# Retention layer followed by a multiplicative feed-forward: heads of a pair swapped in the second output bank from the third step on, a marker copy on VectorE, and a new order of loads and of the first four steps

## Chip, cores and metric

The kernel runs on one core of one Trainium2 chip. The time is device microseconds (us) of one execution. Every duration below is in us unless it is marked ns.

## What is computed

```python
gamma = 1.0 - 2.0 ** (-5.0 - np.arange(H))            # B, H, S, D = 4, 8, 768, 64
for t in range(S):
    state = gamma * state + einsum('bhd,bhe->bhde', k[:, :, t], v[:, :, t])
    y[:, :, t] = einsum('bhd,bhde->bhe', q[:, :, t], state) / sqrt(D)
x = y.transpose(0, 2, 1, 3).reshape(B * S, H * D)      # 3072 tokens x 512
out = ((x @ w1) * (x @ w2)) @ w3 @ w_out               # 512 -> 1024 -> 1024 -> 512
```

## The kernel before, in words

**Tiling.** The recurrence is worked in 12 steps `n` (three for each of four batches), each of 256 tokens. Steps 0 and 1 (`n < EO = 2`) divide the 256 tokens into two chunks `g`, the later ones into four chunks `(s, g)`. `w3 @ w_out` is multiplied out once, into eight tiles W3O, before the first output.

**One step.** `cast` and `cast_v` (L261, L273) turn the loaded fp32 tiles into fp16; q and k are then transposed, by TensorE in `turn`/`turned` (L299, L306) for steps 0 to 2 and by a DMA in `dma_turn` (L292, issue at L295) for the others. `scores` (L319) and `mask` (L342) make the part inside a chunk; `kv` (L357) makes k times v, which `state` (L384) adds up from chunk to chunk. `inter` (L410, matmul L425) multiplies q with the state, `av` (L440, matmul L450) adds the masked scores times v into the same PSUM banks X[n, 0] and X[n, 1], and `x_out` (L456, L467 from step 2 on) scales with a table (YS or YN) and writes the fp16 tile XT. Head pair `a` holds two heads `r`; `inter`, `av`, `kv` and `scores` use 64x64 matmuls. A 64x64 matmul takes its weights from one half of the partitions (the row half of the array) and writes one half of the PSUM partitions (the column half). In `inter` the row half is `r` and so is the column half; the bank is `g`. In `av` the row half is `g`, the column half `r`. Between the two stands `fence` (L432, copy L438): ScalarE reads a few columns of both banks, so that `av` starts only when all of `inter` has been written.

**Feed-forward.** `a_unit` and `b_unit` (L499, L502; matmul L484) multiply XT with W1 and W2 in units of 256 columns. `a_evac` (L490, copy at L59) puts the first on ScalarE; `b_evac` (L494, L62) multiplies it with the second on VectorE into HT. `o_unit` (L528, matmul L532) multiplies HT with W3O, and `o_copy` (L540, L546) scales and writes out.

**What sets the order.** The program is written out by hand (`manual_schedule`): each engine runs its instructions strictly in the order in which the calls stand, and waits where one is not ready. L572 to L838 is a list of calls for the start, steps 0 to 2 and the attention of steps 3 and 4. From L877 on a loop runs over steps 3 to 11. Its first pass (n = 3) only calls `catch_up` (L859) and the feed-forward of step 3. A pass n > 3 is `inter(n)`, `fence(n)`, `ahead(n+1)` (scores and kv of the next step), `av(n)`, `x_out`, `ahead_out` (states and masks of the next step), the transposes of n + 2, loads and casts of n + 3, two `o_unit` of n - 1, and four `a_unit`/`b_unit` pairs.

**Queues.** All transfers, transposing ones too, are issued by SyncE in the order of the calls, on one queue. Loads go into 15 staging buffers `st`, reused in turn. The casts of the loop (`casts`, L842) are on GpSimd ("g"); in the list each call names its engine ("v" VectorE, "s" ScalarE, "g" GpSimd). The eight PSUM banks have the names S0, S1, X0, X1, K, F0, F1, F2; a call that names a bank waits until its last reader is done. `warm` (L562) is a run of matmuls on zeros.

The end of the list, which the prediction uses most:

```python
    o_copy(2, 0)
    state(4, 3)
    scores(4, ("X0", "K"))
    x_out(3, 1)
    o_unit(2, 1, ("F2",))
    cast("q", 5, "s")
    x_out(3, 0)
    state(4, 4)
    mask(4, 1)
    state(4, 5)
    o_copy(2, 1)
    cast("k", 5, "v")
    mask(4, 0)
    cast_v(5, "v")
```

Of the kernel before, what the change touches and what calls it, by code (L numbers as in the profile page):

```python
# [20 lines left out]
def kernel(  # L21
# [86 lines left out]
    def fetch(names):  # L108
# [12 lines left out]
        "r4 wo0 r1 r2 wo1 r5 wo2 r3 r6 k0 r7 wo3 q0 v0 r0 q1 k1 v1 w11 w13 w10 w12 w22 w23 w21 w20 "  # L121
        "v2 v3 k2 q2 k3 v4 q4"
# [10 lines left out]
    LGP = const.tile([128, NP], FP, name="LGP")  # L133
    keep = const.tile([128, 2, 128], FP, name="keep")
# [4 lines left out]
    def numbers():  # L139

        nc.gpsimd.iota(key_i[:, :, :], pattern=[[1, 2], [0, H]], base=1 - 128, channel_multiplier=2)
        nc.gpsimd.iota(
            col_i[:, :, :].rearrange("p g (t j) -> p g t j", t=2), pattern=[[128, 2], [1, 2], [2, 64]],
            base=1 - 128, channel_multiplier=0,
        )
        for h in range(H):
            r = (h % 2) * 64
            nc.gpsimd.memset(LGH[:, h : h + 1], -math.log(gam[h]))
            nc.gpsimd.memset(LGP[r : r + 64, h // 2 : h // 2 + 1], math.log(gam[h]))

# [65 lines left out]
    def late_tables():  # L216
        nc.scalar.activation(VN[:, :, :], vn_x[:, :, :], AF.Exp)
        for p in range(NP):
            nc.scalar.activation(YN[:, :, p, :, :], pos_f[:, :, :, :], AF.Exp, scale=LGP[:, p : p + 1])

# [157 lines left out]


# [30 lines left out]
    def inter(n, tags):  # L410
# [4 lines left out]
        for a in range(NP):  # L415
            for c in cs:
                if (n, c) not in TS:
                    continue
                for r in range(2):
                    if n < EO:  # L420
                        g, o, rhs = c, X[n, c][half(r), a, :], qT[n][half(r), :, a, half(c)]
                    else:
                        s, g = c
                        o, rhs = X[n, g][half(r), a, s * 64 : (s + 1) * 64], qchunk(n, r, a, s, g)
# [7 lines left out]
    def fence(n):  # L432

        for g in range(2):
            if (g, 0) in X[n]:
                s0 = 0 if n < EO or (n, (0, g)) in TS else 1
                t = att.tile([128, NP, 2 - s0], FP, tag=f"fence{g}", name="fence")
                nc.scalar.copy(t[:, :, :], X[n, g][:, :, :].rearrange("p a (s i) -> p a s i", s=2)[:, :, s0:, 0])  # L438

    def av(n):  # L440
        begun = X.pop(n)
        for a in range(NP):
            for t in range(2):
                for g, r in QUARTERS:
# [3 lines left out]
                    else:  # L448
                        o, rhs = X[n, g][half(r), a, t * 64 : (t + 1) * 64], am[n, None, r][half(g), a, t, :]
# [6 lines left out]
    def x_out(n, g):  # L456
# [9 lines left out]
        else:  # L466
            nc.vector.tensor_tensor(  # L467
                XT[n][:, :, :].rearrange("p a (s x) -> p (a s) x", s=2)[:, :, g * 64 : (g + 1) * 64].rearrange(
                    "p k (i t) -> p k t i", t=2
                ),  # L470
                x[:, :, :].rearrange("p a (s t i) -> p (a s) t i", s=2, t=2),
                YN[:, g, :, :, :].rearrange("p a s (t i) -> p (a s) t i", t=2), MULT,
            )
# [99 lines left out]
    warm(8)  # L573
    identity()
    numbers()
    keeps()
    arguments()
    tables()
    cast_w3(4, "v")
    step_decays()  # L580
    turn_w3(4, "S0")
    warm(4)
    late_numbers()
    cast_wo(0, "v")
    turned_w3(4, "s")
    late_arguments()
    w3_mm(4, 0, "S0", first=True)
    warm(7)
    cast_w3(1, "v")
    late_tables()  # L590
    turn_w3(1, "S1")
    warm(3)
    cast_w3(2, "g")
    turned_w3(1, "v")
    turn_w3(2, "X0")
    cast_wo(1, "g")
    w3_mm(1, 0, "S1", first=True)
    turned_w3(2, "s")
    w3_mm(1, 1)
    cast_w3(5, "v")  # L600
    w3_mm(4, 1)
    w3_mm(2, 1, "X0", first=True)
    w3_mm(2, 0)
    cast_wo(2, "g")
    turn_w3(5, "X1")
    turned_w3(5, "s")
    w3_mm(4, 2)
    w3_mm(1, 2)
    cast_w3(3, "s")
    w3_mm(2, 2)  # L610
    w3_mm(5, 2, "X1", first=True)
    cast_w3(6, "v")
    w3_mm(5, 0)
    turn_w3(3, "K")
    turn_w3(6, "F0")
    turned_w3(3, "v")
    w3_mm(5, 1)
    turned_w3(6, "v")
    w3_mm(3, 2, "K", first=True)
    w3_mm(3, 1)  # L620
    cast("k", 0, "v")
    w3_mm(6, 0, "F0", first=True)
    cast_w3(7, "g")
    w3_mm(6, 2)
    turn("k", 0, "F1")
    turn_w3(7, "F2")
    cast_wo(3, "v")
    w3_mm(3, 0)
    turned_w3(7, "s")
    turned("k", 0, "v")  # L630
    w3_mm(5, 3, last=True)
    w3_mm(1, 3, last=True)
    w3_out(5, "s")
    w3_mm(2, 3, last=True)
    cast("q", 0, "v")
    w3_mm(7, 2, "F1", first=True)
    w3_out(1, "s")
    w3_out(2, "v")
    turn("q", 0, "X1")
    w3_mm(4, 3, last=True)  # L640
    turned("q", 0, "v")
    w3_mm(7, 0)
    cast_v(0, "g")
    w3_mm(7, 3)
    w3_out(4, "v")
    scores(0, ("S1", "X0"), 0)
    scores(0, ("S0", "X1"), 1)
    cast_w3(0, "v")
    w3_mm(3, 3, last=True)
    w3_mm(6, 1)  # L650
    mask(0, 0, 1)
    w3_out(3, "s")
    turn_w3(0, "F2")
    mask(0, 1, 1)
    kv(0, ("S0", "K"))
    cast("q", 1, "g")
    mask(0, 0, 0)
    w3_mm(7, 1, last=True)
    w3_mm(6, 3, last=True)
    state(0, 1)  # L660
    w3_out(7, "s")
    turn("q", 1, "S1")
    mask(0, 1, 0)
    w3_out(6, "s")
    inter(0, ("S0", "X1"))
    cast("k", 1, "g")
    state(0, 2)
    fence(0)
    turned_w3(0, "v")
    av(0)  # L670
    state(0, 3)
    turned("q", 1, "v")
    turn("k", 1, "X0")
    w3_mm(0, 2, "K", first=True)
    cast_v(1, "g")
    turned("k", 1, "s")
    x_out(0, 0)
    w3_mm(0, 0)
    w3_mm(0, 3)
    x_out(0, 1)  # L680
    cast_w(W1, "w1", 1, "s")
    scores(1, ("S0", "S1"), 1)
    scores(1, ("X0", "F0"), 0)
    mask(1, 1, 1)
    w3_mm(0, 1, last=True)
    rows(W1, 0, 0, 1, ("X1", "F1"), first=True)
    mask(1, 1, 0)
    w3_out(0, "s")
    cast_w(W1, "w1", 3, "g")
    kv(1, ("S1", "F2"))  # L690
    mask(1, 0, 0)
    rows(W1, 0, 1, 1, ("K", "F0"), first=True)
    state(1, 1)
    rows(W1, 0, 0, 3)
    cast_w(W1, "w1", 0, "g")
    mask(1, 0, 1)
    inter(1, ("S1", "X0"))
    state(1, 2)
    rows(W1, 0, 1, 3)
    fence(1)  # L700
    state(1, 3)
    cast_w(W1, "w1", 2, "s")
    av(1)
    rows(W1, 0, 0, 0)
    x_out(1, 0)
    rows(W1, 0, 1, 0)
    cast_w(W2, "w2", 2, "g")
    x_out(1, 1)
    rows(W1, 0, 0, 2, last=True)
    rows(W1, 0, 1, 2, last=True)  # L710
    rows_out("a", 0, 0, 1, "s")
    rows(W1, 1, 0, 1, ("S0", "S1"), first=True)
    rows_out("a", 0, 1, 1, "s")
    rows(W2, 0, 0, 2, ("X0", "F1"), first=True)
    rows(W1, 1, 0, 0)
    rows_out("a", 0, 1, 0, "s")
    rows(W1, 1, 1, 1, ("F0", "F2"), first=True)
    cast_w(W2, "w2", 1, "g")
    cast_w(W2, "w2", 3, "s")
    rows(W1, 1, 0, 2)  # L720
    rows(W1, 1, 1, 3)
    rows_out("a", 0, 0, 0, "s")
    rows(W2, 0, 0, 3)
    cast_w(W2, "w2", 0, "v")
    rows(W2, 0, 0, 1)
    rows(W2, 0, 1, 3, ("X1", "K"), first=True)
    rows(W2, 0, 1, 2)
    rows(W2, 0, 1, 1)
    rows(W2, 0, 0, 0, last=True)
    cast_v(2, "g")  # L730
    rows(W1, 1, 1, 2)
    rows_out("b", 0, 0, 0)
    rows(W1, 1, 1, 0, last=True)
    rows(W2, 0, 1, 0, last=True)
    rows_out("b", 0, 0, 1)
    rows_out("a", 1, 1, 0, "s")
    rows(W1, 1, 0, 3, last=True)
    rows_out("a", 1, 1, 1, "v")
    rows(W2, 1, 0, 0, ("X0", "F0"), first=True)
    rows_out("a", 1, 0, 0, "s")  # L740
    rows(W2, 1, 0, 2)
    rows_out("b", 0, 1, 0)
    rows(W2, 1, 1, 1, ("S0", "F1"), first=True)
    rows_out("b", 0, 1, 1)
    rows(W2, 1, 1, 2)
    rows(W2, 1, 1, 3)
    cast_v(3, "v")
    rows(W2, 1, 0, 3)
    rows(W2, 1, 0, 1, last=True)
    cast("k", 2, "g")  # L750
    o_unit(0, 0, ("X1",))
    rows_out("a", 1, 0, 1, "v")
    rows_out("b", 1, 0, 0)
    rows_out("b", 1, 0, 1)
    turn("k", 2, "S1")
    o_copy(0, 0)
    cast("q", 2, "v")
    kv(2, ("X0", "K"))
    turned("k", 2, "s")
    rows(W2, 1, 1, 0, last=True)  # L760
    state(2, 1)
    turn("q", 2, "X1")
    state(2, 2)
    o_unit(0, 1, ("F0",))
    rows_out("b", 1, 1, 1)
    turned("q", 2, "s")
    state(2, 3)
    cast("k", 3, "s")
    rows_out("b", 1, 1, 0)
    inter(2, ("S1", "X0"))  # L770
    o_copy(0, 1)
    dma_turn("k", 3)
    fetch("q3 k4")
    scores(2, ("S0", "X1"))
    o_unit(1, 0, ("K",))
    mask(2, 0)
    cast_v(4, "g")
    fence(2)
    mask(2, 1)
    av(2)  # L780
    cast("q", 4, "s")
    kv(3, ("S0", "X1"))
    x_out(2, 1)
    o_unit(1, 1, ("F0",))
    o_copy(1, 0)
    dma_turn("q", 4)
    x_out(2, 0)
    state(3, 1)
    state(3, 2)
    ab["a", 2, 0] = two_blocks(W1, 2, 0, "S1")  # L790
    o_copy(1, 1)
    state(3, 3)
    ab["a", 2, 1] = two_blocks(W1, 2, 1, "X0")
    state(3, 4)
    a_evac(2, 0, ab["a", 2, 0])
    cast("q", 3, "g")
    ab["a", 2, 2] = two_blocks(W1, 2, 2, "S0")
    a_evac(2, 1, ab["a", 2, 1])
    state(3, 5)
    dma_turn("q", 3)  # L800
    ab["a", 2, 3] = two_blocks(W1, 2, 3, "S1")
    a_evac(2, 2, ab["a", 2, 2])
    ab["b", 2, 0] = two_blocks(W2, 2, 0, "S0")
    cast("k", 4, "v")
# [148 lines left out]
```

## Time and profile before

| what | value |
|---|---|
| median of 3 runs | 188.38 us (186.6 to 189.68) |
| the profiled execution, its own time | 187.29 us |
| its span, first to last instruction | 185.6 us |
| granted TensorE clock | 1.000 |
| busy: TensorE, its weight loads, VectorE, ScalarE, GpSimd | 175.7, 125.6, 100.2, 65.7, 56.9 us |
| moved by DMA | 40.76 MB, mean 220 GB/s |

The 1.69 us between 187.29 and 185.6 lie before the first and behind the last instruction. PE is TensorE's matmuls, PEld its weight loads, DVE VectorE, ACT ScalarE, POOL GpSimd, SPq the queue of SyncE that issues the DMAs. In a timeline each line is: start, duration, engine, source line, operation, output and inputs, shapes, count; in brackets the idle time of that engine before it, and what ended the wait. The chain of waits lists the work that ended last, in order of time: start, duration, what. Matmuls are pipelined, so a matmul's duration is longer than the time from its start to the next one's; where the text counts TensorE's work it goes by starts.

### The profile page before, as it was taken

To read this page: it belongs to the slowest core of one execution; us is meant where nothing else is said; L and a number is where in the kernel's file an instruction comes from. 1 tells how busy PE (TensorE), PEld (TensorE's weight loads), DVE (VectorE), ACT (ScalarE), POOL (GpSimd) and SP (SyncE) were. 2 spreads that over 40 slices of the span, in tenths; PEclk is the share of its full clock that TensorE was granted. 3 is DMA by queue.
4 is the path that set the end of the run, shared out by engine and by line. 5 is a ranking of instruction groups with operands and counts; after the bars stand their busy time and mean duration, and the time that the engine had idled before them with its cause. 6 is when DMAs were issued, how large, how long until landed. Compare 5 with 4: busy or idle time off the path is not lost.

```text
span 185.6 us, 5990 instructions
## 1 busy us (share of the span) xinstructions
PE 175.7 (95%) x2606; PEld 125.6 (68%) x2606; DVE 100.2 (54%) x171; ACT 65.7 (35%) x125; POOL 56.9 (31%) x85
## 2 busy tenths in 40 slices
PE   7999989999999988789999999999999999999993
PEld 2555546588765864675886868858678587685872
DVE  2424679625967188548347465373564745634220
ACT  5634414472082604221423323333243241331322
POOL 7860258644204301003425353532614500000000
PEclk9999999999999999999999999999999999999999
DMA  6999999999999989669999899999999996110303
GB/s 215 349 421 359 324 302 325 413 335 193 233 215 196 185 157 257 112 146 255 150 267 178 209 195 216 282 182 245 235 192 289 137 407 260 69 48 2 117 0 113
DMA packets 83578, 40.76 MB, mean 220 GB/s; under 512 B 61408, under 2 KB 78048, under 8 KB 83552
## 3 DMA queue, kind: packets, MB, share of 16 engines
q1 hardware_dynamic: 83552, 40.38, 93.3%
q8 instruction: 20, 0.33, 0.8%
q14 instruction: 6, 0.05, 0.1%
HBM read 29.36 MB, written 6.29 MB: 192 GB/s over the span
## 4 chain that ended last, share of the span: by engine, by line
PE 72%; DMA 16%; SPq 6%; POOL 2%; issue 1%; DVE 1%; ACT 0%; DVEq 0%; POOLq 0%
PE psF L484 32%; PE psF L532 19%; DMA st<-in_v_dram 9%; DMA st<-in_moe_w_dram 7%; SPq L95 3%; PE psF L514 3%; PE psX L425 3%; PE psS L484 2%; PE psX L514 2%; SPq L87 2%; PE psS L514 1%; PE psX L450 1%; PE psS L335 1%; DVE ht L62 1%; POOL v L62 1%
## 5 line engine op out<-in xcount | busy, mean ns | idle before, releaser
L484 PEld LDWEIGHTS <-w 128*128 128x128 f16 x640 | 62.6, 98 | 13.2 <-issue 4.0
L484 PE MATMUL psF<-xt,w 128*128 128x256 f16 x576 | 64.5, 273 | 2.6 <-DVE ht L62 1.9
L62 DVE TENSOR_TENSOR ht<-pa,psF 128x512 f16<-128x512 f32 x39 | 26.7, 686 | 40.5 <-PE psF L484 40.5
L532 PE MATMUL psF<-w3o,ht 128*128 128x512 f16 (+2 forms) x176 | 38.3, 370 | 0.0
L59 ACT COPY pa<-psF 128x512 f32<-128x512 f32 x39 | 22.8, 586 | 41.3 <-PE psF L484 36.7
L532 PEld LDWEIGHTS <-ht 128*128 128x128 f16 x200 | 18.4, 98 | 19.3
L546 ACT ACTIVATE st<-psF 128x512 f32<-128x512 f32 (+2 forms) x19 | 10.9, 575 | 31.0 <-PE psF L532 31.0
L62 POOL TENSOR_TENSOR v<-st,VN 128x1024 f16<-128x1024 f32 x8 | 15.2, 1903 | 17.7 <-DMA st<-in_v_dram 17.7
L59 POOL CAST k<-st 128x1024 f16<-128x1024 f32 x8 | 8.3, 1038 | 33.7 <-DMA st<-in_k_dram 33.7
L467 DVE TENSOR_TENSOR xt<-psX,YN 128x512 f16<-128x512 f32 x18 | 12.2, 727 | 7.4 <-PE psX L450 7.4
L514 PEld LDWEIGHTS <-w 128*128 128x128 f16 x128 | 12.0, 98 | 2.6 <-ACT w L59 0.7
L59 POOL CAST q<-st 128x1024 f16<-128x1024 f32 x8 | 8.3, 1041 | 10.3 <-DMA st<-in_q_dram 9.5
L352 DVE TENSOR_TENSOR am<-psS,keep 128x512 f16<-128x512 f32 x15 | 9.6, 680 | 1.2 <-PE psX L335 1.2
L248 PEld LDWEIGHTS <-w3t 128*128 128x128 f16 x64 | 5.6, 97 | 6.8 <-issue 0.8
L62 POOL TENSOR_TENSOR t<-s,GS 128x256 f16<-128x256 f32 x8 | 5.8, 730 | 13.1 <-DVE s L62 13.1
L514 PE MATMUL psF<-xt,w 128*128 128x256 f16 x56 | 9.7, 273 | 0.0
L565 PE MATMUL psX<-zeros 128*128 128x512 f16 x22 | 7.4, 484 | 1.3 <-DVE zeros L128 1.3
L425 PEld LDWEIGHTS <-t 64*64 64x64 f16 x320 | 6.2, 109 | 2.6 <-issue 2.1
L59 DVE CAST w3h<-st 128x1024 f16<-128x1024 f32 x5 | 4.1, 822 | 6.3 <-DMA st<-in_moe_w_dram 6.3
L425 PE MATMUL psX<-qT,t 64*64 64x64 f16 (+1 forms) x288 | 7.4, 195 | 0.0
L236 PEld LDWEIGHTS <-w3h 128*128 128x128 f16 x64 | 4.2, 103 | 3.5 <-DVE w3h L59 2.4
L484 PE MATMUL psS<-xt,w 128*128 128x256 f16 x48 | 5.7, 272 | 0.8 <-DVE ht L62 0.8
(129 smaller groups left out, 202.9 us busy)
## 6 DMA issues: line engine op xcount, KB each, us to landing
st<-in_moe_w_dram SPq DMA_DIRECT2D x16, 512.0 KB, 8.9
st<-in_q_dram SPq DMA_DIRECT2D x12, 512.0 KB, 5.9
st<-in_v_dram SPq DMA_DIRECT2D x20, 256.0 KB, 5.8
st<-in_k_dram SPq DMA_DIRECT2D x20, 256.0 KB, 5.0
out_dram<-st SPq DMA_DIRECT2D x8, 512.0 KB, 5.5
st<-in_moe_w_out_dram SPq DMA_DIRECT2D x4, 512.0 KB, 7.8
out_dram<-osb SPq DMA_DIRECT2D x3, 512.0 KB, 6.2
st<-in_k_dram SPq DMA_DIRECT2D x2, 512.0 KB, 10.1
```

What stands on the lines that cost most here:

```text
L59: {"v": nc.vector.tensor_copy, "g": nc.gpsimd.tensor_copy, "s": nc.scalar.copy}[eng](dst, src)
L62: (nc.vector if eng == "v" else nc.gpsimd).tensor_tensor(dst, a, b, op)
L95: nc.sync.dma_start(t[:, :], src[i * 128 : (i + 1) * 128, :])
L248: nc.tensor.matmul(acc[f][:, :], lhsT=w3t[f][:, g * 128 : (g + 1) * 128], rhs=WO[i][:, r, :], start=(first and r == 0), stop=(last and r = ...
L352: nc.vector.tensor_tensor(t[:, :, :, :].rearrange("p a s i -> p (a s) i"), ps[:, :, :, :].rearrange("p a s i -> p (a s) i"), keep64[:, :]. ...
L425: nc.tensor.matmul(o, lhsT=TS[n, c][half(r), a, :], rhs=rhs, start=((g, r) not in begun), stop=False, skip_group_check=True,)
L467: nc.vector.tensor_tensor(XT[n][:, :, :].rearrange("p a (s x) -> p (a s) x", s=2)[:, :, g * 64 : (g + 1) * 64].rearrange("p k (i t) -> p k ...
L484: nc.tensor.matmul(ps[:, i, :], lhsT=W[d][:, f * 128 : (f + 1) * 128], rhs=XT[n][:, d, :], start=(i == 0 and d == 0), stop=(i == 1 and d = ...
L514: nc.tensor.matmul(rows_ps[w, n, uh][j // 2][:, j % 2, :], lhsT=W[d][:, f * 128 : (f + 1) * 128], rhs=XT[n][:, d, :], start=(first and j % ...
L532: nc.tensor.matmul(ps[:, :], lhsT=HT[n][:, f, tb * 128 : (tb + 1) * 128], rhs=W3O[f][:, c0:c1], start=(f == 0), stop=(f == 7),)
L546: nc.scalar.activation(o_sb[n][:, tb, c0:c1], o_ps.pop((n, tb, c0, c1))[:, :], AF.Copy, scale=final_scale)
L565: nc.tensor.matmul(ps[:, :], lhsT=zeros[:, 0:128], rhs=zeros[:, :], start=True, stop=True)
```

## The change

- `place` swaps the two heads of a pair in bank g = 1 from step 2 on: in `inter` and `av` the column half there is 1 - r. `inter` then goes through four different pairs of row half and column half, one after the other, instead of two; within a chunk pair the order is now (g, r) = (0, 0), (1, 1), (0, 1), (1, 0).
- `x_out` puts the heads back: for g = 1 it becomes two VectorE instructions on 64 partitions each, for which the table YN is built with swapped rows (LGX: eight more small GpSimd memsets; YN in eight ScalarE activations of half the size).
- In the loop the `fence` copy of bank 1 moves to VectorE, and the last `b_evac` of a step is put behind the next step's `fence` in VectorE's order (`b_last`).
- `catch_up` no longer transposes step 5: both `dma_turn("q", 5)` and `dma_turn("k", 5)` now stand in the list.
- The order of the loads and the list of calls are new from end to end. The calls are nearly the same; `warm` matmuls go from 22 to 25, and several casts change their engine.

```diff
     fetch(
-        "r4 wo0 r1 r2 wo1 r5 wo2 r3 r6 k0 r7 wo3 q0 v0 r0 q1 k1 v1 w11 w13 w10 w12 w22 w23 w21 w20 "
-        "v2 v3 k2 q2 k3 v4 q4"
+        "r3 r6 wo0 r5 q0 r4 wo2 k0 wo1 wo3 r2 v0 r1 r7 k1 q1 v1 w12 w11 r0 w10 w13 w23 w20 w21 w22 "
+        "v2 q2 k2 q5 k3 k4 q3 q4 v3"
     )
...
+    def place(n, g, r):
+        return half(r if n < EO or g == 0 else 1 - r)
...
         for a in range(NP):
-            for c in cs:
-                if (n, c) not in TS:
-                    continue
-                for r in range(2):
+            for c, r in [(c, r) for c in cs for r in range(2)] if n < EO else [
+                ((s, g), r) for s in range(2) for g, r in ((0, 0), (1, 1), (0, 1), (1, 0))
+            ]:
+                if (n, c) in TS:
...
-                        o, rhs = X[n, g][half(r), a, s * 64 : (s + 1) * 64], qchunk(n, r, a, s, g)
+                        o, rhs = X[n, g][place(n, g, r), a, s * 64 : (s + 1) * 64], qchunk(n, r, a, s, g)
...
-                nc.scalar.copy(t[:, :, :], X[n, g][:, :, :].rearrange("p a (s i) -> p a s i", s=2)[:, :, s0:, 0])
+                copy(
+                    "s" if g == 0 else eng, t[:, :, :],
+                    X[n, g][:, :, :].rearrange("p a (s i) -> p a s i", s=2)[:, :, s0:, 0],
+                )
...
-                for g, r in QUARTERS:
+                for g, r in QUARTERS if n < EO else ((0, 0), (1, 0), (0, 1), (1, 1)):
...
+            for to in (slice(0, 128),) if g == 0 else (half(0), half(1)):
+                at = to if g == 0 else slice(64 - to.start, 128 - to.start)
+                nc.vector.tensor_tensor(
+                    xt[to].rearrange("p k (i t) -> p k t i", t=2),
+                    x[at, :, :].rearrange("p a (s t i) -> p (a s) t i", s=2, t=2),
+                    YN[at, g, :, :, :].rearrange("p a s (t i) -> p (a s) t i", t=2), MULT,
+                )
...
     def catch_up():
-        turns(LAST + 2)
         loads(LAST + 3)
         casts(LAST + 3)
...
             inter(n, ("X0", "X1"))
-            fence(n)
+            fence(n, "v")
+            b_last()
...
-            b_unit(n, u, tags[(2 * u + 1) % 3])
+            ps = two_blocks(W2, n, u, tags[(2 * u + 1) % 3])
+            b_last = functools.partial(b_evac, n, u, ps)
+            if u < 3 or n == NS - 1:
+                b_last()
```

The new list begins and ends like this (the middle is left out):

```python
    warm(8, "F2")
    identity()
    step_decays()
    late_numbers()
    numbers()
    warm(3, "F2")
    cast_w3(3, "v")
    turn_w3(3, "S0")
    keeps()
    late_arguments()
    warm(9, "F2")
    arguments()
    late_tables()
    turned_w3(3, "v")
    cast_w3(6, "g")
    cast_wo(0, "v")
    tables()
    turn_w3(6, "S0")
    cast_w3(5, "g")
    w3_mm(3, 0, "S1", first=True)
...
    cast("q", 5, "g")
...
    cast("k", 3, "s")
    rows_out("b", 1, 1, 0)
    inter(2, ("S0", "S1"))
    cast("k", 4, "g")
    scores(2, ("X1", "K"))
    o_copy(0, 0)
    dma_turn("k", 3)
    o_unit(1, 0, ("X0",))
    mask(2, 0)
    fence(2)
    mask(2, 1)
    cast("q", 3, "g")
    av(2)
    o_copy(1, 0)
    o_unit(1, 1, ("X1",))
    x_out(2, 1)
    dma_turn("q", 3)
    fetch("v4")
    x_out(2, 0)
    cast("q", 4, "v")
    ab["b", 2, 3] = two_blocks(W2, 2, 3, "S0")
    o_copy(1, 1)
    dma_turn("q", 4)
    dma_turn("k", 4)
    dma_turn("q", 5)
    fetch("k5 v5")
    ab["a", 2, 2] = two_blocks(W1, 2, 2, "S1")
    cast_v(3, "v")
    ab["a", 2, 1] = two_blocks(W1, 2, 1, "X0")
    a_evac(2, 2, ab["a", 2, 2])
    ab["b", 2, 1] = two_blocks(W2, 2, 1, "S1")
    a_evac(2, 1, ab["a", 2, 1])
    ab["a", 2, 0] = two_blocks(W1, 2, 0, "X0")
    b_evac(2, 1, ab["b", 2, 1])
    ab["b", 2, 2] = two_blocks(W2, 2, 2, "X1")
    a_evac(2, 0, ab["a", 2, 0])
    kv(3, ("S1", "X0"))
    b_evac(2, 2, ab["b", 2, 2])
    ab["a", 2, 3] = two_blocks(W1, 2, 3, "K")
    state(3, 1)
    cast_v(4, "g")
    ab["b", 2, 0] = two_blocks(W2, 2, 0, "X1")
    state(3, 2)
    a_evac(2, 3, ab["a", 2, 3])
    state(3, 3)
    b_evac(2, 3, ab["b", 2, 3])
    scores(3, ("K", "F0"))
    inter(3, ("S1", "F1"))
    mask(3, 0)
    o_unit(0, 1, ("F2",))
    fence(3)
    b_evac(2, 0, ab["b", 2, 0])
    mask(3, 1)
    o_unit(2, 0, ("S0",))
    state(3, 4)
    o_copy(0, 1)
    state(3, 5)
    kv(4, ("X0", "X1"))
    o_copy(2, 0)
    av(3)
    state(4, 1)
    scores(4, ("K", "F0"))
    cast("k", 5, "g")
    x_out(3, 1)
    o_unit(2, 1, ("S0",))
    x_out(3, 0)
    dma_turn("k", 5)
    mask(4, 1)
    cast_v(5, "g")
    o_copy(2, 1)
    mask(4, 0)
    state(4, 2)
    state(4, 3)
    state(4, 4)
    state(4, 5)
```

## Prediction

> **What bounds the kernel now.** I read the page first, then the timeline where TensorE is not full, then one pass of the loop, then the loads.
>
> The page's slices (40 of 4.64 us, busy tenths of TensorE and of the DMA engines):
>
> ```profile
> PE   7999989999999988789999999999999999999993
> ...
> DMA  6999999999999989669999899999999996110303
> ```
>
> TensorE is full except near the start and around slices 14 to 16; the DMA engines are full until about 74 us and after 83. From 84 to 182 the loop is bound by TensorE; up to 84, TensorE and the loads both bind.
>
> The timeline from 60 to 80 us, VectorE, ScalarE and TensorE:
>
> ```profile
> 65.43 0.69 DVE L59 CAST k<-st 128x1024 f16<-128x1024 f32 x1 [4.41 <-DMA st<-in_k_dram]
> ...
> 66.77 1.03 PE L484 MATMUL psS<-xt,w 128*128 128x256 f16 x8 [0.76 <-DVE ht L62]
> ...
> 72.06 1.05 ACT L59 CAST q<-st 128x1024 f16<-128x1024 f32 x1 [0.72 <-DMA st<-in_q_dram]
> ...
> 73.86 3.65 PE L484 MATMUL psF<-xt,w 128*128 128x256 f16 x32 [0.69 <-ACT osb L546]
> ...
> 75.69 0.69 DVE L59 CAST k<-st 128x1024 f16<-128x1024 f32 x1 [2.23 <-DMA st<-in_k_dram]
> ...
> 77.57 1.22 DVE L62 TENSOR_TENSOR v<-st,VN 128x1024 f16<-128x1024 f32 x1 [0.58 <-DMA st<-in_v_dram]
> ...
> 79.44 3.65 PE L484 MATMUL psF<-xt,w 128*128 128x256 f16 x32 [1.92 <-DVE ht L62]
> ```
>
> All three TensorE waits have one form: a cast of a late load (k4, q5, k5 and v5) stands in the strict order of VectorE or ScalarE, a PSUM reader stands behind it, and TensorE waits for the bank. From the first unit of step 2 (59.74) to inter(4) (83.03) are 23.3 us. By the distance of starts the work in it is 16 units of 0.874 (14.0), two o_unit of 1.74 (3.5) and 1.6 of attention: 19.1. So 4.2 us are waits.
>
> One loop pass, step 5, where inter, scores, kv and av follow each other:
>
> ```profile
> 95.00 0.63 PE L425 MATMUL psX<-qT,t 64*64 64x64 f16 x28
> 95.44 0.22 PE L335 MATMUL psS<-qT,kT 64*64 64x64 f16 x2
> ...
> 95.52 0.42 PE L335 MATMUL psS<-qT,kT 64*64 64x64 f16 x28
> 95.75 0.25 ACT L438 COPY fence<-psX 128x8 f32<-128x8 f32 x2 [0.94 <-PE psX L425]
> ...
> 95.78 0.20 PE L374 MATMUL psK<-v,k 64*64 64x64 f16 x1
> ...
> 101.94 0.69 DVE L62 TENSOR_TENSOR ht<-pa,psF 128x512 f16<-128x512 f32 x1 [1.04 <-PE psF L484]
> ```
>
> Inter takes 0.44 for 28 starts (16 ns each), the 28 scores from 95.52 to 95.78 take 9.3 ns each. VectorE has 1.04 us to spare before its first ht.
>
> The loads' landings, by the casts that waited for them:
>
> ```profile
> 49.13 1.04 POOL L59 CAST k<-st 128x1024 f16<-128x1024 f32 x1 [3.04 <-DMA st<-in_k_dram]
> ...
> 50.99 0.69 DVE L59 CAST q<-st 128x1024 f16<-128x1024 f32 x1 [0.39 <-DMA st<-in_q_dram]
> ...
> 56.14 1.90 POOL L62 TENSOR_TENSOR v<-st,VN 128x1024 f16<-128x1024 f32 x1 [5.97 <-DMA st<-in_v_dram]
> 58.98 1.05 ACT L59 CAST q<-st 128x1024 f16<-128x1024 f32 x1 [3.38 <-DMA st<-in_q_dram]
> ```
>
> They land one after another: a q costs 50.99 - 49.13 = 1.86; k3 and v4 cost 56.14 - 50.99 = 5.15, 2.58 each; q4 came 2.84 behind v4, 1.0 late, with k3's transpose issued at 55.00.
>
> **The change, part by part.** *The start.* GpSimd has more ahead of its first cast: from the identity's end (1.37) GS 1.94, late numbers 1.61, iotas 0.45, 24 small memsets (16 took 1.50, so 2.25), keep 1.98, so it casts r6 at 9.6 and r5 at 10.7 (1.04 each). VectorE's argument tables wait for LGH until 7.7, then it turns out r3. TensorE's 20 warm-ups end at about 8.3 and it has nothing until r6 is cast (10.7). Before, three W3 tiles were turned by 10.9; now two by 11.3. I then walked the new list with the rows' durations (VectorE 0.61 to 0.69 per cast, ScalarE 1.01, turn 0.44, w3_mm 0.44, landings by position in the queue, 1.25 to 1.3 per weight block as between 10.55 and 13.11). The chain cast, turn, turned out, product has no slack up to r7, and the first W1 row group starts at 34.4. Set against before at 35.25, where its own last wait in this part ends, it lacks W3 tile 0 (turn 0.44, eight products of 0.218) and two row groups (0.87) and is ahead by inter(1) (0.35): 2.7 of work, so it is 34.4 + 2.7 - 35.25 = 1.85 late.
>
> *34.4 to the first unit of step 2.* Before needed 24.49 from 35.25 to 59.74. The new list adds those 2.7 and puts off o_unit(0, 1) and kv(3) (1.74 + 0.30); inter(2) saves 0.13; the third x_out part makes XT come 0.3 behind o_unit(1, 1). 34.4 + 24.49 + 2.7 - 2.04 - 0.13 + 0.3 = 59.7.
>
> *59.7 to inter(4).* The work is 19.1 + 2.04 - 0.1 = 21.0: inter(4) at 80.7 if nothing waits. What can wait now: k4, q5, k5 and v5 are cast on GpSimd, with no PSUM reader behind them, so the three old waits go. But cast q4 and v3 are on VectorE ahead of four b_evac. v3 is ninth instead of second: v2 q2 k2 q5 k3 k4 q3 is 4 x 2.58 + 3 x 1.86 = 15.9 against 14.76 for the six up to v4 at 56.14, so 57.3; q4 59.1, v3 61.7, and 1.0 later if k3's transpose runs among them as before: 62.7. Its cast ends at 63.9, b_evac(2, 1) at 64.5, just when kv(3) wants bank S1 (64.6). No cost, no slack. Next late are the transposes on SyncE's queue, k3 q3 (v4) q4 k4 q5. Scores(4) needs k4's. Before they started without waiting at 70.91, behind the same transfers but without q5's load (1.86): 72.8 at most. From there 0.3 + o_unit(2, 1) 1.74 + eight units 6.99 gives inter(4) at 81.8. Ends 80.7 and 81.8; I take 81.5, nearer to the loads, which fill their engines. Gain 83.03 - 81.5 = 1.5. K5's transpose no longer stands with q5's behind v5: scores(5) wants it at about 82. A transpose costs 1.46 of the queue (v7 waited for at 100.53, k8 at 106.03, two transposes and a k between: (5.50 - 2.58) / 2); 72.8 + 1.46 (q5) + 2 x 2.58 (k5, v5) = 79.4 for v5, whose GpSimd cast (1.9) ends at 81.3, and 80.9 for k5's transpose: cover of 0.7 us, less if the loads slip.
>
> *The loop, steps 4 to 11.* Inter and scores together take 0.78 (95.00 to 95.78); 64 starts at 9.3 ns are 0.60. Bounds: 0 (the old rate) and 0.18, 0.13 in steps 6 and 9, which have 24 matmuls: at most 1.3. The new order visits all four quadrants like scores, so I take 1.0 in all. The fence needs inter's last start + 0.19 + 0.06 + 0.17 = 0.42, less than scores and kv behind it (0.6): no wait, and its move to VectorE gains nothing but in step 11. VectorE pays 0.62 (third x_out part; back-to-back distance) of its 1.04: 0.4 left. b_last starts about 0.6 later and ends near 96.4; o_unit reads its two rows of HT with the seventh matmul, 6 x 0.218 after 95.95: hidden. If that cover goes, a late ht holds a bank that is wanted 1.75 later: still nothing. Warm-ups, fence and ACT's halved tables otherwise lie in waits.
>
> A rule that speaks against the loop's gain: by the Trainium skill, "TensorE: Matmul & The Clock Gate", Part 3, a weight load overlaps a running matmul only if its row group differs. The new order's row halves are 0, 1, 1, 0, the scores' 0, 1, 0, 1. By that rule the loop gains nothing and the sum ends 1.0 higher. No row here shows such an order.
>
> The same page (Part 1) throttles TensorE after an idle window of about 3.4 us; the idle after the warm-ups is 2.4, below it. In this trace the first eight warm matmuls took 3.60, the last seven 1.67. If the gate closed, an estimate from the page would be some 1.7 more in the start.
>
> **Sum.** 187.29 (the profiled execution, 1.69 of it outside the span) - 1.5 - 1.0 = 184.8. That execution was 1.1 quicker than the median, 188.38, from which it would be 185.9. I say 185.3.
>
> **Rivals.**
> *More gain*: the loads keep ahead and the quadrants reach the scores' rate: (83.03 - 80.7) + 1.3 = 3.6, 184.2 by the same middle, less if the start is quicker than walked. For it: DMA is only at 6 tenths in slices 16 and 17. Against: full before.
> *Heads swapped, no faster*: the 16 ns stay; only the 1.5 is left: 186.3. For it: neighbours share a row or column half, as never before.
> *The start is not made up*: another 1.5 lost in the walk's chain before 34.4, inter(4) at 83: 186.8. For it: chain without slack.
> *Slower*: v3's cast holds VectorE. It stands ahead of b_evac(2, 1), which frees S1 for kv(3); each us that v3 lands after 62.8 is one on the path. From 65.3 on the whole gain of 2.5 is gone. If transposes get in front of the last two loads at their dearest (4.8 from issue to landing, the median), v3 lands at 67.5 and the time is 190. Against: it was issued ahead of them.
>
> **How the numbers follow.** Chances: forecast 0.45 (own range 184.2 to 186.4), more gain 0.22, no faster 0.12, start 0.11, slower 0.10. A measurement tells about 2% from no change: 3.8 us, so faster is below 184.6. That takes most of the second case and a quarter of the first: 0.32. Slower by 2% (192.2) needs the last case and a bad start: 0.08. Range: down past 184.2 by 1.4 (the start's uncertainty), up to where half of the last case is in: 182.8 to 188.8.
>
> **What would show it.** Right: first W1 row group near 34.4; no idle over 0.3 on TensorE from there to 58; no PE wait for ht behind a cast between 59 and 80; scores(4) near 72.5 waiting for kT; inter(4) near 81.5; inter's starts 10 to 13 ns apart; loop passes of 11.85 instead of 12.0. Wrong: v3's cast after 64, VectorE's spare time before the first ht at zero, a fence that TensorE waits for, or a loop pass no shorter.

## The result, and the profile after

The kernel with the change takes 186.13 us (median of 20 runs, 184.52 to 187.09), the kernel before 188.33 (20 runs beside them, 186.43 to 190.65). Five of the runs of before are in a slower state that none of after's shows; the ratio leaves them out and is 0.9905, 95% interval 0.9876 to 0.9935. So the change gains about 1.8 us or 1%: clear of zero, and inside the 2% that was called no change. The profiled execution took 186.98 (span 185.2). Against the profiled one of before, 187.29, that is only 0.3, because after's lies 0.85 above its median and before's 1.0 below. So the two traces show where time is won and lost, and the runs the size of the gain; what spreads the runs of before over 4 us was not looked for.

The slices of after's page (4.63 us each):

```profile
PE   7769999999999899999999999989999999999993
...
PEclk9969999999999999999999999999999999999999
DMA  5999999999989999699899899999999990110203
```

Two things are new. The dip of TensorE around slices 14 to 16 has gone, and in the third slice the granted clock is at 6 tenths, where before had full speed throughout. The mean over the execution is 0.990. That is the usual case: 15 of after's 20 runs have a mean clock of 0.988 to 0.991, five of 0.999 to 1.000.

The start on TensorE, from after's timeline:

```profile
11.03 1.04 PE L241 MATMUL psS<-ident,w3h 128*128 128x128 f16 x8 [2.85 <-POOL w3h L60]
```

The granted clock us by us, from after's windows (start and end, length, then busy us of TensorE, its weight loads, VectorE, ScalarE and GpSimd, granted clock, DMA share, GB/s):

```profile
10.00:11.00 1.00, 0.00 (x0) 0.00 (x0) 0.00 (x0) 1.00 (x5) 1.00 (x2) 0.88 1.02 401
11.00:12.00 1.00, 0.97 (x9) 0.97 (x10) 0.00 (x0) 1.00 (x3) 0.96 (x1) 0.50 0.98 371
...
13.00:14.00 1.00, 1.00 (x6) 0.47 (x5) 0.99 (x2) 0.00 (x0) 0.00 (x0) 0.50 1.17 338
14.00:15.00 1.00, 1.00 (x13) 0.76 (x12) 0.00 (x0) 0.43 (x1) 0.00 (x0) 0.92 1.04 401
```

TensorE stands idle for 2.85 us until r6 is cast, and in this idle time the clock goes to half. From the 0.88 and the 0.92 the half clock lasts from 10.76 to 14.16, 3.4 us. The turn of r6 takes 1.04 for eight transposes, against 0.61 at full clock.

The part from 58 to 80 us (timeline):

```profile
58.81 2.21 DVE L482 TENSOR_TENSOR xt<-psS,YN 64x512 f16<-64x512 f32 x3 [0.99 <-PE psS L462]
...
60.91 0.68 DVE L60 CAST q<-st 128x1024 f16<-128x1024 f32 x1
...
61.07 1.92 PE L497 MATMUL psS<-xt,w 128*128 128x256 f16 x16 [0.59 <-DVE xt L482]
61.50 1.22 DVE L63 TENSOR_TENSOR v<-st,VN 128x1024 f16<-128x1024 f32 x1
```

VectorE's timeline at the end of that stretch:

```profile
73.40 0.42 DVE L63 TENSOR_TENSOR t<-psX,t 128x256 f16<-128x256 f32 x1 [2.04 <-PE psX L379]
73.86 1.47 DVE L482 TENSOR_TENSOR xt<-psF,YN 64x512 f16<-64x512 f32 x2
75.34 0.72 DVE L482 TENSOR_TENSOR xt<-psS,YN 128x512 f16<-128x512 f32 x1
```

And TensorE's first unit of step 3, behind them:

```profile
76.12 7.15 PE L497 MATMUL psF<-xt,w 128*128 128x256 f16 x64 [0.42 <-DVE xt L482]
```

The three old waits (0.76, 0.69, 1.92) are gone. In their place TensorE waits twice for `x_out`, 0.59 and 0.42: three VectorE instructions instead of two stand between `av` and the first unit of steps 2 and 3. The cast of the slower rival, v3's at 61.50, shows no wait for its load at all. And no load is what the end of this stretch waits for; k5's cast was waiting for TensorE:

```profile
73.30 1.04 POOL L60 CAST k<-st 128x1024 f16<-128x1024 f32 x1 [1.06 <-PE psX L379]
76.61 1.90 POOL L63 TENSOR_TENSOR v<-st,VN 128x1024 f16<-128x1024 f32 x1 [2.27 <-DMA st<-in_v_dram]
```

These two are on GpSimd, and nothing on the path stands behind them. inter(4) starts at 83.20, before at 83.03. The timeline of before:

```profile
83.03 0.63 PE L425 MATMUL psX<-qT,t 64*64 64x64 f16 x28
```

And of after:

```profile
83.20 0.45 PE L434 MATMUL psX<-qT,t 64*64 64x64 f16 x32
```

One pass of the loop, step 5 (timeline):

```profile
94.95 0.45 PE L434 MATMUL psX<-qT,t 64*64 64x64 f16 x32
...
95.23 0.55 PE L340 MATMUL psS<-qT,kT 64*64 64x64 f16 x32
...
95.57 0.17 DVE L60 COPY fence<-psX 128x8 f32<-128x8 f32 x1 [1.50 <-PE psX L434]
...
96.67 2.21 DVE L482 TENSOR_TENSOR xt<-psX,YN 128x512 f16<-128x512 f32 x3 [0.34 <-PE psX L462]
...
101.83 0.67 DVE L63 TENSOR_TENSOR ht<-pa,psF 128x512 f16<-128x512 f32 x1
```

The 32 starts of `inter` now take 95.23 - 94.95 = 0.28, 8.7 ns each, where 28 took 0.44. The fence makes nobody wait here. The first ht of the pass shows no wait any more: VectorE's spare 1.04 is used up.

The chain of waits for the pass of step 7 (start, duration, what):

```profile
118.80 0.38 PE psX L434 x32
119.17 0.29 PE psS L340 x30
...
120.00 1.19 PE psF L545 x5
121.19 0.82 issue
122.01 2.55 PE psF L545 x11
124.56 5.46 PE psF L497 x50
```

In the middle of an `o_unit` TensorE stands for 0.82 us without waiting for anything that the profile shows ("issue"). The passes last 11.89, 11.89, 12.75, 11.88, 11.75, 11.74 and 11.70 (first unit to first unit, from step 4 on); the 12.75 is this one. Before they took 12.01, 12.01, 11.98, 11.98, 11.94, 11.97 and 11.98.

The end of the loop is read from the last 24 output products, the x24 group at the end of the chain. Before:

```profile
178.93 3.49 PE psF L532 x24
```

After:

```profile
178.61 3.49 PE psF L545 x24
```

From inter(4) to this group it is 178.93 - 83.03 = 95.90 before and 178.61 - 83.20 = 95.41 after, or 94.59 without the 0.82. So the loop gains 1.31 and one stop takes 0.82 of it back.

### The profile page after: what moved, and what is told of

Same layout as the page of the kernel before. It is cut to its first block, busy times and chain, and to the rows that moved or that the text cites. A ratio compares the mean times of both kernels' runs of the same rounds, so it can differ in the third digit from the quotient of the medians.

```text
span 185.2 us, 5993 instructions
## 1 busy us (share of the span) xinstructions
PE 174.4 (94%) x2609; PEld 124.3 (67%) x2609; DVE 112.3 (61%) x191; ACT 67.0 (36%) x122; POOL 53.5 (29%) x90
## 4 chain that ended last, share of the span: by engine, by line
PE 85%; DVE 5%; POOL 5%; issue 2%; ACT 1%; DVEq 0%; POOLq 0%; ACTq 0%
PE psF L497 34%; PE psF L545 19%; PE psX L253 4%; PE psS L253 3%; PE psS L527 3%; PE psF L527 2%; DVE xt L482 2%; PE psX L497 2%; PE psX L434 2%; PE psX L462 2%; PE psS L497 2%; DVE am L351 1%; PE psS L340 1%; PE psX L527 1%; PE psX L545 1%
## 5 line engine op out<-in xcount | busy, mean ns | idle before, releaser
L497 PE MATMUL psF<-xt,w 128*128 128x256 f16 x576 | 64.3, 273 | 0.4 <-DVE xt L482 0.4
L545 PE MATMUL psF<-w3o,ht 128*128 128x512 f16 (+2 forms) x168 | 36.6, 369 | 0.8 <-issue 0.8
L60 ACT COPY pa<-psF 128x512 f32<-128x512 f32 x37 | 21.7, 586 | 34.6 <-PE psF L497 34.4
L482 DVE TENSOR_TENSOR xt<-psX,YN 64x512 f16<-64x512 f32 (+1 forms) x24 | 17.4, 727 | 1.7 <-PE psX L462 1.4
L60 POOL CAST q<-st 128x1024 f16<-128x1024 f32 x9 | 9.6, 1069 | 16.2 <-DMA st<-in_q_dram 14.7
L253 PE MATMUL psX<-wo,w3t 128*128 128x512 f16 x32 | 8.9, 380 | 0.4 <-ACT w3t L60 0.2
L578 PE MATMUL psF<-zeros 128*128 128x512 f16 x25 | 7.5, 442 | 1.3 <-DVE zeros L129 1.3
L527 PE MATMUL psS<-xt,w 128*128 128x256 f16 x48 | 8.2, 273 | 0.4 <-DVE w L60 0.4
L60 DVE COPY fence<-psX 128x8 f32<-128x8 f32 x8 | 1.3, 166 | 11.5 <-PE psX L434 11.5
L253 PE MATMUL psS<-wo,w3t 128*128 128x512 f16 x24 | 7.5, 421 | 0.0
L527 PE MATMUL psF<-xt,w 128*128 128x256 f16 x40 | 6.5, 273 | 0.0
```

Source lines behind the costliest of these rows:

```text
L60: {"v": nc.vector.tensor_copy, "g": nc.gpsimd.tensor_copy, "s": nc.scalar.copy}[eng](dst, src)
L253: nc.tensor.matmul(acc[f][:, :], lhsT=w3t[f][:, g * 128 : (g + 1) * 128], rhs=WO[i][:, r, :], start=(first and r == 0), stop=(last and r = ...
L482: nc.vector.tensor_tensor(xt[to].rearrange("p k (i t) -> p k t i", t=2), x[at, :, :].rearrange("p a (s t i) -> p (a s) t i", s=2, t=2), YN ...
L497: nc.tensor.matmul(ps[:, i, :], lhsT=W[d][:, f * 128 : (f + 1) * 128], rhs=XT[n][:, d, :], start=(i == 0 and d == 0), stop=(i == 1 and d = ...
L527: nc.tensor.matmul(rows_ps[w, n, uh][j // 2][:, j % 2, :], lhsT=W[d][:, f * 128 : (f + 1) * 128], rhs=XT[n][:, d, :], start=(first and j % ...
L545: nc.tensor.matmul(ps[:, :], lhsT=HT[n][:, f, tb * 128 : (tb + 1) * 128], rhs=W3O[f][:, c0:c1], start=(f == 0), stop=(f == 7),)
```

## The experiments

The theory after this reading: the swap gains 1.3 in the loop, and its third `x_out` part costs 1.0 of that in steps 2 and 3, so what the whole change gains is the list. Rivals: the list's gain is lost in the start and the swap is what pays; the wait at 121.19 belongs to the swap; the fast `inter` comes from its order of row halves, not from the four quadrants. The runs stand in three groups, each on one chip: e1 to e4, e5 to e7, and e8 to e10, with medians of the kernel before of 188.34 (23 runs), 187.77 (11) and 188.72 (11). Between groups the ratios to before are compared.

**e1: the swap alone.** Before's loads, list of calls and `catch_up`; after's functions and loop.

> The list of calls and the loads of before, with the swap, the split x_out, the fence on VectorE and the late b_evac of the change. Theory (the swap gives about 1.2 us in the loop, the new list the rest): loop passes of 11.85 instead of 12.0 us, inter's 32 starts in 0.28 us, inter(4) within 0.4 us of 83.0, time 1.0 to 1.4 us below the kernel before. Rival (the new list alone brings the gain, the swap's longer VectorE work eats what inter saves): time within 0.3 us of before.

Measured: 187.3 (12 runs), ratio 0.9968 [0.9932, 1.0004]. The old waits are all there (waits, TensorE):

```profile
PE psF L497 <- DVE ht L63: 1.7, 1, 1.7
PE psF L497 <- ACT osb L559: 0.9, 1, 0.9
...
PE psS L497 <- DVE ht L63: 0.4, 1, 0.4
```

With them stands a wait of 0.3 for xt. Seven passes take 83.30 instead of 83.87, 0.57 less, with an "issue" wait of 0.23 among them. The swap by itself is at most a gain of 0.7%. By the ratio that is 0.6 us, between what the theory (1.0 to 1.4) and the rival (0.3) had asked for, so this run decides for neither.

**e2: the list alone.** After, with the swap taken out everywhere.

```diff
     def place(n, g, r):
-        return half(r if n < EO or g == 0 else 1 - r)
+        return half(r)
...
-            for c, r in [(c, r) for c in cs for r in range(2)] if n < EO else [
-                ((s, g), r) for s in range(2) for g, r in ((0, 0), (1, 1), (0, 1), (1, 0))
-            ]:
+            for c, r in [(c, r) for c in cs for r in range(2)]:
...
-            for to in (slice(0, 128),) if g == 0 else (half(0), half(1)):
+            for to in (slice(0, 128),):
```

> The changed kernel with only the swap undone: inter's old order and halves, x_out in two instructions, YN from LGP; the new list, the fence on VectorE and the late b_evac stay. Theory: loop passes back at 12.0 us, inter's 32 starts in 0.44 us, but XT of steps 2 and 3 some 0.6 us earlier each, so inter(4) near 82.4 instead of 83.3; time 0.5 to 1.0 us below the kernel before. Rival (the swap gives nothing): time equal to the changed kernel or below, 1.8 us or more under before.

Measured: 185.35 (6 runs), ratio 0.989 [0.9848, 0.9933]: the list alone gives what the whole change gives, as the rival had it. Its timeline of TensorE:

```profile
59.74 1.91 PE L495 MATMUL psS<-xt,w 128*128 128x256 f16 x16
...
81.39 0.63 PE L432 MATMUL psX<-qT,t 64*64 64x64 f16 x28
```

No wait for xt; inter(4) at 81.39, which is 1.64 before the kernel before and 1.81 before after. The passes are the old ones, about 12.0, so the swap does give something in the loop, which the rival had denied. The granted clock of the profiled execution is 1.000: the idle time behind the warm-ups was 2.22 here, because the warm-ups ended later.

**e3: the clock gate kept open.** `warm(9, "F2")` becomes `warm(21, "F2")` in after.

> The changed kernel with 21 instead of 9 warm-up matmuls ahead of the wait for r6, 2.6 us of work in an idle stretch. Theory (the idle from 8.2 to 11.0 closed TensorE's clock: granted 0.83 from 10 to 20 us, transposes of 0.13 us instead of 0.055): granted clock 1.00 from 10 to 20 us, first W1 row group near 34.4 instead of 35.25, time 0.3 to 0.9 us below the changed kernel. Rival (VectorE's masks and casts set when the row groups can go on): first row group earlier, but the third group of W1, after w10's cast, still at 38.5, time unchanged.

Measured: 185.67 (12 runs), ratio 0.9897 [0.9863, 0.993]. The clock from 10 to 20 us is 1.00. The first W1 row group comes at 34.92 instead of 35.25, the first unit of step 2 at 60.38 instead of 61.07: the closed gate cost 0.7 on that path. The third row group comes at 37.79, not at 38.5 as the rival had it. The time, 0.46 under after's, is not told apart from it, but after's own runs agree: the 15 with a clock of 0.988 to 0.991 have a median of 186.3, the five with 0.999 or more 185.5, and none of the 12 runs of e3 is below 0.999. An "issue" wait of 0.96 falls in the pass of step 7 here too.

**e4: the keep table later.** In after, GpSimd makes the mask table `keep` behind its first two casts.

```diff
-    keeps()
     late_arguments()
...
     cast_w3(5, "g")
+    keeps()
```

> The changed kernel with GpSimd's keep table (2.2 us) made behind its casts of r6 and r5 instead of ahead of them. Theory (GpSimd's first cast at 9.9 sets the whole start): r6 cast at 7.7, its turn at 8.8, clock 1.00 throughout, first W1 row group at 33 to 34, inter(4) 1.0 to 2.0 us earlier, time 0.8 to 1.8 us below the changed kernel. Rival (from there on the loads' landings set the pace): r5 and q0 follow no earlier, first row group not before 34.5, time within 0.4 us of the changed kernel.

Measured: 183.44 (6 runs), ratio 0.9788 [0.9747, 0.983]: 2.7 below after's median, 2.2 by the ratios, more than the theory's 0.8 to 1.8. Timeline of TensorE:

```profile
9.09 0.62 PE L241 MATMUL psS<-ident,w3h 128*128 128x128 f16 x8 [0.93 <-POOL w3h L60]
...
32.67 0.39 PE L527 MATMUL psS<-xt,w 128*128 128x256 f16 x2
```

The idle time is 0.93 instead of 2.85, the clock stays at 1.0, the first W1 row group comes at 32.67, 2.6 earlier, and inter(4) at 80.43, 2.8 earlier. What limited the start was GpSimd's queue ahead of its first cast, not the loads; some 0.7 of the gain is the clock that now stays open (e3). The waits for xt are unchanged (0.59 and 0.42), the "issue" wait is 0.09.

**e5: the swap only from step 4 on.** e4, with steps 2 and 3 unswapped; the loop's rows get a second table, YX, and steps 2 and 3 use YN in one `x_out` instruction per bank.

```diff
-        return half(r if n < EO or g == 0 else 1 - r)
+        return half(r if n < 4 or g == 0 else 1 - r)
...
-            for to in (slice(0, 128),) if g == 0 else (half(0), half(1)):
+            swap = g == 1 and n >= 4
+            for to in (half(0), half(1)) if swap else (slice(0, 128),):
```

> The kernel with the keep table behind the casts, and the swap from step 4 on only: steps 2 and 3 keep inter's old order and a single x_out instruction for bank 1 (a table YN unswapped for them, a second one, YX, for the others). Theory (the split x_out costs 1.0 to 1.3 us where TensorE waits for XT in the list, steps 2 and 3, and nothing in the loop): no TensorE wait for xt, step 3's first unit at 72.0 to 72.5 instead of 73.35, loop passes as short as with the swap everywhere (11.75 to 11.9), time 0.8 to 1.2 us below e4_keeps. Rival (those waits hide another, a load or a bank): step 3's first unit moves by less than 0.4 us.

Measured: 183.13 (6 runs), ratio 0.9761 [0.9715, 0.9808]. The waits for xt are gone, but the first unit of step 3 comes only 0.62 earlier than in e4 (72.73), not the 0.85 and more that was expected: the second table lengthens ScalarE's part of the start by 0.4 (its tables end at 10.7 instead of 10.3), and inter(2) starts at 53.34 instead of 52.94. From there to inter(4) it is 26.47 instead of 27.49, and that is the 1.02 of the two waits. An "issue" wait of 0.38 is in this run. By the ratios the time is 0.5 below e4, less than the 0.8 to 1.2 of the theory and not told apart from it. v3's cast now does wait for its load:

```profile
60.97 1.22 DVE L63 TENSOR_TENSOR v<-st,VN 128x1024 f16<-128x1024 f32 x1 [2.09 <-DMA st<-in_v_dram]
```

It costs TensorE nothing.

**e6: another order of row halves.** e4, with `inter` in the order (g, r) = (0, 0), (0, 1), (1, 0), (1, 1): the row halves are then 0, 1, 0, 1, as before the change; only the column halves differ from before.

> The kernel with the keep table behind the casts, and inter's order (g, r) = (0,0), (0,1), (1,0), (1,1): the four quadrants as in the change, but the row halves alternate 0, 1, 0, 1 and two neighbours write one bank. Theory (four quadrants in turn are what counts): 32 starts of inter in 0.28 us, time within 0.4 us of e4_keeps. Rival (the order of the row halves matters, as the page's rule has it): starts quicker than 8.7 ns apart, time below e4_keeps by 0.2 us or more; if the shared bank of two neighbours matters instead, starts 12 to 16 ns apart and up to 1.3 us above.

Measured: 184.54 (6 runs), ratio 0.9839 [0.9784, 0.9894]. Timeline of TensorE:

```profile
93.23 0.45 PE L434 MATMUL psX<-qT,t 64*64 64x64 f16 x32
93.50 0.46 PE L340 MATMUL psS<-qT,kT 64*64 64x64 f16 x32
```

32 starts in 0.27, 8.4 ns each, the same as with rows 0, 1, 1, 0. With the same order of rows but two quadrants they took 16 ns. It is the four quadrants. The time is 1.0 above e4 by the ratios, not within 0.4, though the intervals overlap. Its inter(4) is at 81.47, 1.0 later than e4's, and inter(2), the first that the edit touches, is already 1.0 late (53.98 against 52.94). Up to there the two programs are the same: e6 has a wait of kv for v (0.4) and an "issue" wait (0.4) there. So the delay in this trace does not come from the order; why the median of the six runs is higher too stays open. Another "issue" wait, of 0.3, is in the pass of step 7.

**e7: both fences on ScalarE.** e4, with `fence(n)` as before and `b_evac` in its old place.

> The kernel with the keep table behind the casts, with both fence copies on ScalarE and the last b_evac of a step back in its old place. Theory (the fence ends before kv does, on one engine or two): loop passes within 0.05 us of e4_keeps, in step 11, where nothing covers it, 0.08 us more; time within 0.3 us. Rival (with inter shortened two copies in a row, 0.25 us, end after kv): TensorE waits for the fence in each pass, 0.05 to 0.1 us each, 0.4 to 0.8 us in all.

Measured: 183.94 (6 runs), ratio 0.9824 [0.9753, 0.9896], not told apart from e4. The passes up to step 10 have no fence wait. Only in step 11, where no scores and kv of a next step stand between, does the second copy show (timeline of TensorE):

```profile
163.97 0.19 PE L462 MATMUL psX<-am,v 64*64 64x64 f16 x1 [0.33 <-ACT fence L60]
164.35 0.44 PE L462 MATMUL psX<-am,v 64*64 64x64 f16 x31 [0.19 <-ACT fence L60]
```

The same place in e4:

```profile
163.82 0.45 PE L462 MATMUL psX<-am,v 64*64 64x64 f16 x32 [0.33 <-ACT fence L60]
```

One matmul of `av` runs by itself and the other 31 follow 0.38 later. From inter(11) to the first unit of step 11 e7 takes 4.99 (163.20 to 168.19) and e4 4.61 (163.05 to 167.66). So the marker on VectorE is worth 0.38, in one step; 0.08 was expected.

**e8, e9, e10: with and without the swap, start cleared.** e8 is e2 with `keeps()` moved as in e4, e9 is e4 once more, e10 is e5 once more.

> The new list without the swap, and the keep table made behind GpSimd's first two casts: the counterpart of the run with the keep table moved, which has the swap. It tells what the swap is worth by itself once the start is out of the way. Theory A (the swap gives 1.2 in the loop, 0.1 to 0.15 a pass, and loses 1.0 of it where TensorE waits for x_out's third part in steps 2 and 3): passes of 12.0, no wait for xt, the first unit of step 3 about 1 us earlier, and a time within 0.5 of the kernel with the swap, 183.2 to 184.0. Rival B (the swap is a net gain once the start is clear): 184.5 or more. Rival C (the swap is a net loss, also by waits for instructions that only kernels with it show): 182.9 or less.

> The run with the keep table moved once more, on the same chip as the two beside it, so that the three are compared over the same runs of the kernel before. Both theories: 0.979 of the kernel before, 183.0 to 184.0.

> The run with the swap from step 4 on once more, on the same chip. Theory A (the waits for xt in steps 2 and 3 are what the swap pays, so leaving these two steps unswapped keeps its gain): 0.3 to 1.0 below both kernels beside it. Rival (what the two waits cost is given back at once by a later wait for v3): within 0.3 of the kernel with the swap from step 2.

| | e8: no swap | e9: swap from step 2 | e10: swap from step 4 |
|---|---|---|---|
| median of 6 runs, us | 183.91 | 183.58 | 183.22 |
| ratio to before, interval | 0.9776 [0.9731, 0.9821] | 0.9762 [0.9707, 0.9816] | 0.9747 [0.9697, 0.9796] |
| inter(2) | 52.78 | 53.19 | 53.53 |
| inter(4) | 79.25 | 80.69 | 80.02 |
| x24 group of step 11 | 175.66 | 175.64 | 174.46 |
| "issue" wait in step 7's pass | 0.42 | 0.31 | none |

From inter(2) to inter(4), e8 takes 26.47, e9 27.50, e10 26.49: 1.03 for swapping steps 2 and 3, which are the waits of 0.60 and 0.42. From inter(4) to the x24 group, without the "issue" waits, e8 takes 95.99, e9 94.64, e10 94.44: 1.35 to 1.55 for the swap in the loop. Over all twelve profiled executions the same stretch is 95.8 to 96.0 in the three without the swap (before, e2, e8) and 94.3 to 94.9 in the nine with it, 1.3 between the means. So e9 starts inter(2) 0.41 later than e8, loses 1.03, gains 1.35 and stops 0.11 less, and both come to the x24 group within 0.02 of each other. The waits of TensorE in e9 (us in total, times, longest):

```profile
PE psS L497 <- DVE xt L482: 0.6, 1, 0.6
PE psF L497 <- DVE xt L482: 0.4, 1, 0.4
```

The same view of e8:

```profile
PE psF L543 <- issue: 0.4, 1, 0.4
PE psX L460 <- ACT fence L60: 0.3, 1, 0.3
```

The last fence shows also that the "issue" wait isn't the swap's: e8 has no swap and has the wait. Nor is its length the kernel's: 0.09 and 0.31 in two executions of one (e4, e9), 0.38 and none in two of another (e5, e10). So the rival that the swap is a net loss by such waits falls, and theory A, that the two nearly balance, holds. The traces put e10 1.2 ahead of the other two, which are equal. The medians are only 0.3 to 0.4 apart, and the intervals overlap: e10 against e9, and e9 against e8, are not told apart by time.

## Why the prediction was right or wrong

The forecast, 185.3, was 0.8 under the median, and the median lies in its range; the 1% gained is what it had called no change that can be told. Its mechanism was right in its two gains, and wrong in where they would be lost. From one profiled execution to the other the sum said 187.29 to 184.8, and 186.98 came, 2.2 more; that the median of the runs lies so near the forecast is in part luck. By its steps:

- **The three old waits go: right.** None is left, and e2 shows their worth with the list alone: inter(4) at 81.39, where the prediction had 81.5.
- **But 81.5 was reached by two errors that cancel.** The work from the first unit of step 2 to inter(4) was counted as 21.0; in e2 and e8, which wait for nothing there, it is 21.65 (81.39 - 59.74 and 79.25 - 57.60). The prediction's own lines could have told: their three waits add up to 3.37, not to the 4.2 that it took for waits, so before's work was 19.9 and not 19.1. Units and o_units, priced at their closest distance, make up most of that (14.5 instead of 14.0, 3.7 instead of 3.5). In return I let the loads hold back scores(4) to near 72.5 and moved 0.8 up for that. No load held it. The transposes ran in time, and the next late thing was VectorE.
- **`x_out`'s third part: the size failed.** I priced it at 0.3 in step 2, nothing in step 3. It is 0.59 and 0.42 (e8 against e9: 1.03). In step 3 the path is state(4, 1) at 73.40, then three parts to 76.06, each of them needed by the first unit, and o_unit(2, 1) in front covers only some of it. I had costed the third part in the loop, where two o_units cover it, and not asked what covers it in the list, where one does.
- **The start: the gate step failed.** I had 2.4 of idle time, under the window of 3.4 that I took from the Trainium skill, "TensorE: Matmul & The Clock Gate", Part 1, and so no half clock. It was 2.85, because GpSimd came to its first cast at 9.94 and not at 9.6 (its 24 small memsets took 3.2, where I had 2.25), and the clock was halved 10.76 - 8.19 = 2.57 us after the last warm-up matmul ended. The measurement decides: an idle time shorter than the page's window was enough here, and one of 2.22 (e2) was not. The page does say that the window runs freely, so that its phase counts. The price, 0.7 (e3), is less than half of the 1.7 that the prediction had estimated from the page.
- **The first W1 row group at 34.4: 35.25.** Without the half clock it was 34.55 (e2) and 34.92 (e3, whose longer warm-ups put the turn of r6 off to 11.55). A wait of 0.36 at 38.55 for VectorE's cast of w10, slowed by a cast on GpSimd (last section), comes on top; e3 and e4 do not have it.
- **The sum at inter(4).** 81.5 + 0.85 (start) + 0.36 (w10) + 0.29 (0.59 instead of 0.3) + 0.42 (step 3) = 83.4; measured 83.20. So in the profiled execution the start and the list gain nothing, and the rival "the start is not made up", with inter(4) at 83 and 186.8, is what that execution did: 83.20 and 186.98. It had named only a part of the place; half of the loss is behind the start.
- **The loop: right, a little low.** Predicted 1.0 with bounds 0 and 1.3; it is 1.31 without the stop at 121.19, 1.35 to 1.55 in e9 and e10, at and above the upper bound. The quadrants reached the rate of `scores`. By the rule of the same page, Part 3, that a weight load overlaps only with a different row group, there should have been no gain from rows 0, 1, 1, 0; at 8.7 ns a start, and 8.4 in e6 for rows 0, 1, 0, 1, the runs here do not agree with it.
- **VectorE's spare time: half right.** I charged it 0.62 and left 0.4. The third part lengthens `x_out` from 1.34 to 2.21, 0.87. Where before had 1.53 to spare, 0.41 and 0.52 are left (1.42 in the pass with the stop); where it had 1.04, none is recorded. The prediction had named that as a sign of being wrong; but, as its own text on the loop says, a late ht cost nothing: TensorE shows no wait for ht.
- **The slower rival (v3's cast): fell.** It did not wait in after, and in e5 it waited 2.09 without a cost.
- **The fence: right.** No wait in the passes; in step 11 the move to VectorE gains 0.38 (e7).
- **Not foreseen: the stop of 0.82 in the middle of an o_unit.** It is in most executions with the new list and in e1, and not in the profiled one of before. What it goes by is told in the last section.

## What to carry to other kernels

A split of one instruction into two is costed at every place where it runs: the loop had cover for it and the hand-made start had not, and the start took back most of what the loop had gained (1.03 of 1.35 in e9). Leave such a change out of the steps where its result is needed at once (e10, by its trace; its time is not told apart from e9's). When the start idles the matrix engine, look at the queue of the engine that makes the first operand: a table that nobody needs yet, ahead of a cast, cost more (2.2 us by the ratios, the halved clock included) than the whole change brought (1.8).

## What the runs showed of the hardware

**64x64 matmuls.** With all four quadrants in turn (pairs of row half and column half) the 32 of `inter` start 8.4 to 8.7 ns apart, with two 16 ns apart; the order of the row halves makes no difference (e6). In steps 6 and 9, where `inter` has only 24 matmuls, it is 10.7 ns against 16.

**A VectorE cast beside a GpSimd cast.** The same fp32 to fp16 cast takes 0.67 to 0.69 on VectorE and 1.04 on GpSimd alone. Where the two overlap, the one that started first keeps its time and the other is held up. In after GpSimd is first, and VectorE's cast takes 1.34 (timeline):

```profile
36.91 1.04 POOL L60 CAST w<-st 128x1024 f16<-128x1024 f32 x1 [1.25 <-DMA st<-in_moe_w_dram]
...
37.16 1.34 DVE L60 CAST w<-st 128x1024 f16<-128x1024 f32 x1
```

In e4 VectorE is first by 0.03, and GpSimd's cast takes 1.54 (timeline):

```profile
36.97 0.67 DVE L60 CAST w<-st 128x1024 f16<-128x1024 f32 x1
37.00 1.54 POOL L60 CAST w<-st 128x1024 f16<-128x1024 f32 x1 [3.40 <-DMA st<-in_moe_w_dram]
```

The other executions agree. Behind 36 us, VectorE's cast takes 1.18 to 1.55 in the five where GpSimd is first (after, e2, e3, e5, e9) and ends 0.55 after GpSimd's in each. In the five where VectorE is first (e4, e6, e7, e8, e10) it takes 0.67 and GpSimd's 1.43 to 1.54. Which of them is first changes between two executions of one kernel (e4, e9).

**The stop of TensorE.** Of the eleven profiled executions with the change or a part of it, eight have one stop of TensorE in the pass of step 7, 0.09 to 0.96 us long, for which the profile names no releaser; e2, e7 and e10 have none. The traces hold two things that it goes by. It always stands ahead of the same matmul by count, the 1759th of TensorE, whatever that is in the program: in e3, with 12 warm-ups more, it is one of `av`, in the others one of an `o_unit`. And it ends 2.60 to 2.82 us after the same 16 KB instruction fetch began (after: fetch at 119.33, stop from 121.19 to 122.01). In before, e2, e7 and e10 that matmul comes 2.87 to 3.45 us after the fetch anyway, and there is no stop. So it looks like a wait for instructions, set by the place in the instruction stream; no run was made to move it on purpose.
